# One pair of weights first, 66 pieces of attention alone on all PSUM banks, then FFN passes with the other weights converted under them

## The chip, the cores and the metric

The kernel runs on one core of a Trainium2 chip. The time is the device time of one execution in microseconds. Before the change it is 1069.12 us, the median of three runs (1068.13 to 1069.79).

## The reference: local and global attention, then an ELU feed-forward layer

```python
# q_l, k_l, v_l: (8, 8, 512, 64); q_g, k_g, v_g: (8, 8, 32, 64); w_in: (512, 2048); w_out: (2048, 512); all float32
s_g = scale * matmul(q_g, concat([k_g, k_l]).T)           # 32 global rows of each head see everything
out_g = matmul(sm(s_g), concat([v_g, v_l]))
s_ll = where(abs(i - j) <= 32, scale * matmul(q_l, k_l.T), -1e9)   # local rows see a band
s_l = concat([scale * matmul(q_l, k_g.T), s_ll])          # and the 32 global keys
out_l = matmul(sm(s_l), concat([v_g, v_l]))
x = concat([out_g, out_l]) as (4608 tokens, 512)
h = x @ w_in
g = where(h > 0, h, exp(min(h, 0)) - 1)
return g @ w_out
```

The weights arrive as eight-byte numbers (read as pairs of int32) and are turned into float32 and then into two float16 parts by the kernel itself.

## The kernel before

**Attention** is one generator of pieces (lines 357 to 559). A batch has ten slots: two global ones ("g", the 32 global queries of four heads against all keys) and eight local ones ("l", 128 local queries of four heads). Each slot takes four pieces, named S, T, U and V. Piece S of a local slot multiplies queries and keys (L434, `stage_s`), VectorE adds the mask and takes the maximum (L445), ScalarE takes the exponential (L452), VectorE and GpSimd normalise (L456, L457, L459). Two slots later pieces T and U transpose the probabilities on TensorE (L470) and copy them out of PSUM (L473), and one slot later still piece V multiplies them with the values (L489), whose result ScalarE copies to `xr` (L493). A global slot has the products of L385 and the softmax of L393 to L407. All of these use the PSUM pool `ps_a`, four banks. Eight batches make 80 slots and 323 pieces.

**The FFN** works on 17 blocks of 256 tokens: two to each batch, and one (the last) of all global rows. For a block, `split_x` finds the largest element (a transpose on TensorE, L101, then small VectorE steps) and writes the float16 parts `xh` (ScalarE, L285) and `xl` (VectorE, L288). A **pass** is one block with one pair of the 16 slices of 128 hidden units: 24 matmuls of L213 into PSUM `h`, the ELU (L221 and L222 on ScalarE, L223 on GpSimd, L228 on VectorE), its two float16 parts (L230, L231), and two passes later 12 matmuls of L255 into PSUM `acc`. That is 8 passes to a block and 136 in all. `h` and `acc` have two banks each, so that the eight banks are 2 + 2 + 4. A pass is eight steps of the generator `ffn_stream`.

**The weights** are converted in 16 units: for each of the eight pairs one unit of `w_in` and one of `w_out` (`unit`, L124). A unit loads 1 MB (L129, L132), and then runs steps on ScalarE (L141, L154 or none, L165), GpSimd (L142) and VectorE (L146, L147, L149, L152 for `w_in`, small steps, L168); a unit of `w_in` also has a transpose on TensorE (L101, the tile `cm`). The pairs come in groups: "a" is pair 0, "b" pair 1, "c" pairs 2 and 3, "d" pairs 4 to 7. When a group is converted, `tables` makes its scale tables (one transpose of `wm_a`, `wm_b` and so on, L101); with "d" comes "f", the table of all pairs. Until "f" exists, a block is done group by group: the partial sum of a group goes to DRAM (`od`, L267), and the next group loads it (L248) and adds it (L263). Afterwards a block goes through all eight pairs at once.

**The order.** The main loop (L571) takes the pieces of attention in turn. At piece i it starts a unit of a group where `CONV` says so (group "a" from piece 0 every 4 pieces, "b" from 22 every 6, "c" from 38 every 4, "d" from 54 every 4), and then as many FFN steps as `pace` asks for: none up to piece 30, then a ramp to piece 70, and from there 3.2 steps a piece (128 steps to the 40 pieces of a batch). Work that is deferred (`defer`) stands a number of ticks later; a tick is one piece or one FFN step. Every engine runs its instructions in the order that this gives, with some local reordering by the scheduler; all loads and stores go through one queue, SP's.

Of the kernel before, what the change touches and what calls it, by code (L numbers as in the profile page):

```python
# [10 lines left out]
F32 = mybir.dt.float32  # L11
# [10 lines left out]
DM, DF = 512, 2048  # L22
# [11 lines left out]
FFN0, FFN1, FFNLAG = 30, 70, 42  # L34
CONV = {"a": (0, 4), "b": (22, 6), "c": (38, 4), "d": (54, 4)}
# [11 lines left out]
def attn_ffn(ctx: ExitStack, tc: tile.TileContext, qT, qgT, kT, vT, w_in, w_out, mask, out):  # L47
# [36 lines left out]


# [28 lines left out]
    def load_weights(group):  # L114
        lo, hi = GROUPS[group]
        for p in range(lo, hi):
            for m in range(2):
                unit(m, p)
                yield
        defer(9, lambda: tables(group))  # L120
        if hi == NP:
            defer(10, lambda: tables("f"))

    def unit(m, p):  # L124
# [48 lines left out]
        lag = 3 if m else 12 if now[0] < 4 else 6  # L173
# [26 lines left out]
    def ffn_stream():  # L200
# [127 lines left out]
        left = 0  # L328
        while left <= NBL:
            load()  # L330
            job = job or choose()
            if job is None:
                yield True
                continue
            cur, job = job, None
            group, blk = cur[:2]
            lo, hi = GROUPS[group]
            for p in range(lo, hi):
                load()
                yield from ffn1(cur, p)  # L340
                if len(pend) > LAG2:
                    yield from ffn2()
                if p == hi - 1:
                    job = choose()
            if group in "df":
                del xs[blk]
                left += 1
# [9 lines left out]
    def attention():  # L357
# [69 lines left out]
        def stage_s(st, g, t):  # L427

            sp = [ps_a.tile([P, 512], F32, name="pa") for _ in range(2)]
# [35 lines left out]
        def stage_t(st, g, t, j):  # L465
# [6 lines left out]
            copy = nc.vector.tensor_copy if "f" in tab or (j and "a" in tab) else nc.scalar.copy  # L472
            copy(st["pt", g, t][:, 2 * j:2 * j + 2, :, 0:P], tp.rearrange("p (r i q) -> p r i q", r=2, i=2))  # L473

        def stage_v(st, g, t):
# [7 lines left out]
            pv = ps_a.tile([P, 512], F32, name="pa")  # L483
# [78 lines left out]
    spb = 4 * 10  # L562
    per = 2 * NP * 8
    f = ffn_stream()
    lw = [(load_weights(g), *CONV[g]) for g in CONV]
    done = 0

    def pace(i):
        return (i - FFNLAG) / spb * per

    for i, _ in enumerate(attention()):  # L571
        for units, first, step in lw:
            if i >= first and (i - first) % step == 0:
                next(units, None)
        want = pace(i) if i >= FFN1 else pace(FFN1) * (i - FFN0) / (FFN1 - FFN0)
        if done >= want:
            tick()
        while done < want:
            if next(f):
                tick()  # L580
                break
            done += 1
            tick()
# [60 lines left out]
```

## Time and profile before

| | |
|---|---|
| three runs | 1068.13, 1069.12, 1069.79 us |
| profiled execution | 1068.29 us, its span 1066.2 us |
| busy: PE / DVE / ACT / POOL | 994.4 / 568.4 / 526.0 / 296.4 us |
| mean granted TensorE clock | 0.965 |
| moved between DRAM and the core | 81.78 MB |

PE is TensorE, DVE VectorE, ACT ScalarE, POOL GpSimd; PEclk is the granted clock of TensorE as a share of full speed. "Busy" of PE is the union of its matmuls, at whatever clock they ran.

### The profile page before, as it was taken

How to read it: one execution, taken by the hardware profiler on the slowest of the kernel's cores; microseconds unless marked ns; L12 is line 12 of the kernel's file. 1: busy time of each engine (PE TensorE's matmuls, PEld its weight loads, DVE VectorE, ACT ScalarE, POOL GpSimd, SP SyncE). 2: the span in 40 equal slices, each digit the busy share in tenths (PEclk: the TensorE clock that was granted, in tenths of full speed). 3: DMA queues.
4: the chain of work that ended last, by engine and by line, in shares of the span. 5: the costliest groups of instructions: out<-in, count | busy, mean ns of one | idle time of the engine just before them, and what ended most of it. 6: DMA issues, size and time to landing. Idle time of an engine off the chain costs nothing.

```text
span 1066.2 us, 18867 instructions
## 1 busy us (share of the span) xinstructions
PE 994.4 (93%) x7182; PEld 690.5 (65%) x7182; DVE 568.4 (53%) x1669; ACT 526.0 (49%) x1246; POOL 296.4 (28%) x549
## 2 busy tenths in 40 slices
PE   5686985999999999999999999999999999999996
PEld 4464653666666766766676766676676767676663
DVE  5889689753465545454545455544555454433221
ACT  4666566653344445544544455444554454444342
POOL 3463524251222222222222132222222222211110
PEclk7886897999999999999999999999999999999998
DMA  7555356321143101310022102210131000000000
GB/s 289 163 168 193 128 194 227 90 91 44 50 144 120 45 21 65 95 45 26 31 76 82 52 11 94 80 46 14 65 101 41 20 31 22 20 21 20 1 20 21
DMA packets 39154, 81.78 MB, mean 77 GB/s; under 512 B 3864, under 2 KB 5912, under 8 KB 39064
## 3 DMA queue, kind: packets, MB, share of 16 engines
q1 hardware_dynamic: 39064, 80.58, 23.0%
q8 instruction: 57, 0.93, 0.4%
q14 instruction: 33, 0.27, 0.1%
HBM read 65.36 MB, written 15.20 MB: 76 GB/s over the span
## 4 chain that ended last, share of the span: by engine, by line
PE 77%; DVE 12%; ACT 5%; POOL 3%; issue 2%; DMA 1%; SPq 0%; POOLq 0%; ACTq 0%; DVEq 0%
PE h L213 32%; PE acc L255 29%; PE pa L489 6%; PE pa L434 4%; PE pa L470 4%; DVE p L445 2%; ACT p L452 2%; PE pa L385 2%; DVE cu L147 1%; POOL g L223 1%; DVE g L228 1%; DVE cu L149 1%; POOL p L459 1%; DVE gl L231 1%; ACT xh L285 1%
## 5 line engine op out<-in xcount | busy, mean ns | idle before, releaser
L213 PE MATMUL h<-xh,winh 128*128 128x256 f16 x1088 | 298.4, 275 | 17.0 <-ACT xh L285 15.9
L213 PE MATMUL h<-xl,winh 128*128 128x256 f16 x1088 | 298.3, 274 | 3.4 <-DVE xl L288 3.4
L213 PE MATMUL h<-xh,winl 128*128 128x256 f16 x1088 | 298.3, 274 | 0.0
L213 PEld LDWEIGHTS <-winh 128*128 128x128 f16 x2176 | 211.3, 98 | 58.9 <-issue 15.4
L255 PE MATMUL acc<-wouth,gh 128*128 128x512 f16 x544 | 206.8, 380 | 1.0 <-ACT o L266 1.0
L255 PE MATMUL acc<-woutl,gh 128*128 128x512 f16 x544 | 206.2, 379 | 0.0
L255 PE MATMUL acc<-wouth,gl 128*128 128x512 f16 x544 | 206.2, 379 | 0.0
L459 POOL TENSOR_SCALAR p<-p,sm 128x224 f32<-128x224 f32 x256 | 125.2, 507 | 265.8 <-ACT g L221 135.2
L223 POOL TENSOR_SCALAR g<-g,xs 128x512 f32<-128x512 f32 x136 | 95.8, 704 | 339.6 <-ACT g L222 324.1
L230 ACT CAST gh<-g 128x512 f16<-128x512 f32 x136 | 83.9, 617 | 207.4 <-DVE g L228 207.3
L228 DVE SCALAR_TENSOR_TENSOR g<-h,kk_f,g 128x512 f32<-128x512 f32 x104 | 78.1, 751 | 194.5 <-POOL g L223 194.4
L452 ACT ACTIVATE p<-p,m 128x224 f32<-128x224 f32 x256 | 120.1, 471 | 100.2 <-DVE m L448 99.9
L255 PEld LDWEIGHTS <-gh 128*128 128x128 f16 x1088 | 101.7, 98 | 93.0 <-issue 14.6
L221 ACT ACTIVATE g<-h,xs 128x512 f32<-128x512 f32 x136 | 92.7, 682 | 132.1 <-PE h L213 127.5
L231 DVE TENSOR_TENSOR gl<-g,gh 128x512 f16<-128x512 f32 x136 | 94.9, 698 | 45.0 <-ACT gh L230 44.0
L213 PEld LDWEIGHTS <-winl 128*128 128x128 f16 x1088 | 107.1, 98 | 18.0 <-issue 4.8
L445 DVE CUSTOM_DVE_ANT_0 p<-pa,msk 128x224 f32<-128x224 f32 x256 | 87.6, 384 | 24.5 <-PE pa L434 24.5
L255 PEld LDWEIGHTS <-gl 128*128 128x128 f16 x544 | 53.2, 98 | 63.7 <-issue 1.1
L470 PE MATMUL pa<-ident,p 128*128 128x128 f32 x512 | 79.7, 282 | 9.7 <-ACT pt L425 4.5
L222 ACT ACTIVATE g<-g 128x512 f32<-128x512 f32 x136 | 85.7, 630 | 3.6
L473 DVE COPY pt<-pa 128x512 f32<-128x512 f32 x110 | 74.7, 679 | 23.4 <-PE pa L470 22.4
L489 PE MATMUL pa<-pt,v 128*64 128x160 f32 (+2 forms) x1024 | 85.4, 311 | 0.6 <-DVE xglob L500 0.3
(148 smaller groups left out, 968.3 us busy)
## 6 DMA issues: line engine op xcount, KB each, us to landing
v<-vT SPq DMA_DIRECT2D x64, 256.0 KB, 2.7
k<-kT SPq DMA_DIRECT2D x32, 448.0 KB, 4.2
out<-o SPq DMA_DIRECT2D x34, 256.0 KB, 2.0
raw<-w_in SPq DMA_DIRECT2D x8, 1024.0 KB, 5.5
q<-qT SPq DMA_DIRECT2D x32, 256.0 KB, 4.8
raw<-w_out SPq DMA_DIRECT2D x8, 1024.0 KB, 5.2
od<-o SPq DMA_DIRECT2D x24, 256.0 KB, 2.1
o<-od SPq DMA_DIRECT2D x24, 256.0 KB, 3.0
```

The lines of the kernel that those rows point to most:

```text
L213: nc.tensor.matmul(h[:, j, :], wt[:, c, f], xt[:, c, :], start=k == 0, stop=k == 11)
L221: nc.scalar.activation(g, hf, AF.Relu, scale=sc[:, p:p + 1])
L222: nc.scalar.activation(g, g, AF.Exp, scale=-1.0)
L223: nc.gpsimd.tensor_scalar(g, g, -1.0, sc[:, NP + p:NP + p + 1], ALU.add, ALU.mult)
L228: nc.vector.scalar_tensor_tensor(out=g, in0=hf, scalar=kk[:, p:p + 1], in1=g, op0=ALU.mult, op1=ALU.max)
L231: defer(1, lambda: nc.vector.tensor_sub(gl, g, gh))
L255: nc.tensor.matmul(acc[t], gt[:, s], wt[:, f, :], start=p == first and j == 0 and k == 0, stop=p == last and j == 1 and k == 2)
L445: nc.vector.tensor_tensor_reduce(out=p[:, 0:KW], in0=sp[r][:, j * KW:(j + 1) * KW], in1=msk[:, mi, :], op0=ALU.add, op1=ALU.max, scale=1.0 ...
L452: nc.scalar.activation(ps[i][:, 0:KW], ps[i][:, 0:KW], AF.Exp, bias=m[:, 1, i:i + 1], scale=scale, accum_out=s[:, 0, i:i + 1])
L459: nc.gpsimd.tensor_scalar(ps[i][:, 0:KW], ps[i][:, 0:KW], s[:, 1, i:i + 1], 1.0, ALU.mult, ALU.mult)
L470: nc.tensor.transpose(tp[:, (2 * r + i) * P:(2 * r + i + 1) * P], ps[2 * j + r][:, i * P:(i + 1) * P], ident)
L489: nc.tensor.matmul(pv[64 * r:64 * r + 64, j * GW:j * GW + w], v[keys, 2 * j + i, r, :], pt[keys, 2 * j + r, i, 0:w], start=i == 0, stop=i ...
```

## The change: where conversions, attention and FFN steps stand

The first pair (group "a") is converted at pieces 0 and 4 as before. Up to piece 58 nothing else is converted, and up to piece 66 no FFN step is taken; `lead` is true for this time. While it is, piece S takes its two banks from `acc` in every second slot, piece V takes its bank from `h`, and VectorE copies only the second half of the transposed probabilities. `ffn_stream` meanwhile only splits the blocks that are ready. From piece 58 on, a counter starts the next unit after every 14 credits: a piece gives 2, an FFN step 1. The pace is 180 FFN steps between pieces 66 and 112, and 670 between 112 and 320. After the lead and until table "f" exists, ScalarE copies both halves of the transposed probabilities (before, VectorE took one of them once "a" was there). The scale tables are deferred by 14 and 15 ticks behind the start of a group's last unit (before: 9 and 10 behind the unit that followed). The work itself is the same: 323 pieces, 136 passes, 16 units, four blocks that are done group by group.

```diff
-FFN0, FFN1, FFNLAG = 30, 70, 42
-CONV = {"a": (0, 4), "b": (22, 6), "c": (38, 4), "d": (54, 4)}
+PACE = ((0, 0), (66, 0), (112, 180), (320, 850))
+CONV = 14
...
+    lead = [True]
...
                 unit(m, p)
+                if (m, p) == (1, hi - 1):
+                    defer(14, lambda: tables(group))
+                    if hi == NP:
+                        defer(15, lambda: tables("f"))
                 yield
-        defer(9, lambda: tables(group))
-        if hi == NP:
-            defer(10, lambda: tables("f"))
...
-        lag = 3 if m else 12 if now[0] < 4 else 6
+        lag = 3 if m else 10 if lead[0] else 6
...
+        while lead[0]:
+            load()
+            yield True
         while left <= NBL:
...
-            sp = [ps_a.tile([P, 512], F32, name="pa") for _ in range(2)]
+            if lead[0] and np_[0] % 8 == 0:
+                sp = [ps_o.tile([P, DM], F32, name="acc") for _ in range(2)]
+            else:
+                sp = [ps_a.tile([P, 512], F32, name="pa") for _ in range(2)]
...
-            copy = nc.vector.tensor_copy if "f" in tab or (j and "a" in tab) else nc.scalar.copy
+            copy = nc.vector.tensor_copy if "f" in tab or (j and lead[0]) else nc.scalar.copy
...
-            pv = ps_a.tile([P, 512], F32, name="pa")
+            if lead[0]:
+                pv = ps_h.tile([P, 2, BLK], F32, name="h").rearrange("p a b -> p (a b)")
+            else:
+                pv = ps_a.tile([P, 512], F32, name="pa")
...
-    spb = 4 * 10
-    per = 2 * NP * 8
     f = ffn_stream()
-    lw = [(load_weights(g), *CONV[g]) for g in CONV]
-    done = 0
+    units = (u for g in "abcd" for u in load_weights(g))
+    done = credit = 0
     def pace(i):
-        return (i - FFNLAG) / spb * per
+        for (i0, d0), (i1, d1) in zip(PACE, PACE[1:]):
+            if i < i1:
+                break
+        return d0 + (d1 - d0) * (i - i0) / (i1 - i0)
+    def convert(n):
+        nonlocal credit
+        credit += n
+        if credit >= CONV:
+            credit -= CONV
+            next(units, None)
     for i, _ in enumerate(attention()):
-        for units, first, step in lw:
-            if i >= first and (i - first) % step == 0:
-                next(units, None)
-        want = pace(i) if i >= FFN1 else pace(FFN1) * (i - FFN0) / (FFN1 - FFN0)
+        lead[0] = i < PACE[1][0]
+        if i in (0, 4):
+            next(units)
+        elif i >= PACE[1][0] - 8:
+            convert(2)
+        want = pace(i)
+        if lead[0]:
+            next(f)
         if done >= want:
             tick()
         while done < want:
...
             done += 1
+            convert(1)
             tick()
```

Lines of the changed kernel lie 4 to 14 further down: L101 is L105 there, L213 is L218, L434 is L445, L445 is L456, L470 is L481, L489 is L503.

How this moves the instructions is shown at three places. The first is TensorE's list in the first batch, one local slot (S, the transposes T and U, and V of an earlier slot). Before:

```order
L434 MATMUL pa<-k,q 128x224 x4
L419 MATMUL pa<-ident,pg 128x128
L470 MATMUL pa<-ident,p_81 128x128 x2
L470 MATMUL pa<-ident,p_82 128x128 x2
L470 MATMUL pa<-ident,p_83 128x128 x2
L470 MATMUL pa<-ident,p_84 128x128 x2
L489 MATMUL pa<-pt,v 64x160 x8
```

And now:

```order
L445 MATMUL acc<-k,q 128x224 x4
L427 MATMUL pa<-ident,pg 128x128
L481 MATMUL pa<-ident,p_85 128x128 x2
L481 MATMUL pa<-ident,p_86 128x128 x2
L481 MATMUL pa<-ident,p_87 128x128 x2
L481 MATMUL pa<-ident,p_88 128x128 x2
L503 MATMUL h<-pt,v 64x160 x2
```

The products of S stand in `acc` here and the values of V in `h`; the transposes keep `pa`.

The second place is VectorE's list where the first unit of pair 1 is converted (`cu` is the weight being built, `p` and `m` are the masked scores and maxima of attention). Before, it stands among attention pieces of the first batch:

```order
L146 TENSOR_SCALAR cu<-cu 128x1024
L445 ISA p_85,m<-pa,msk 128x224
L445 ISA m 128x1
L147 SCALAR_TENSOR_TENSOR cu<-raw,cu 128x1024
L456 TENSOR_SCALAR sm<-sm 128x4
L445 ISA p_86,m<-pa,msk 128x224
L445 ISA m 128x1
L149 SCALAR_TENSOR_TENSOR cu<-raw,cu 128x1024
L457 RECIPROCAL sm<-sm 128x4
L445 ISA p_87,m<-pa,msk 128x224
L445 ISA m 128x1
L152 TENSOR_REDUCE cm<-cu 128x1
```

Now most units stand among passes (`g`, `gl`), as this one of pair 2, well behind the lead:

```order
L151 TENSOR_SCALAR cu<-cu 128x1024
L152 SCALAR_TENSOR_TENSOR cu<-raw,cu 128x1024
L233 SCALAR_TENSOR_TENSOR g<-h,kk_a,g 128x512
L154 SCALAR_TENSOR_TENSOR cu<-raw,cu 128x1024
L236 TENSOR_TENSOR gl<-g,gh 128x512
L233 SCALAR_TENSOR_TENSOR g<-h,kk_b,g 128x512
L166 TENSOR_SCALAR cm<-cm 128x1
L100 TENSOR_SCALAR pwo<-cm 128x1
L168 RECIPROCAL cm<-pwo 128x1
L169 TENSOR_SCALAR cm<-cm 128x1
L236 TENSOR_TENSOR gl<-g,gh 128x512
```

The units have moved from between attention pieces to between the steps of passes.

The third place is ScalarE's list in the steady part, where a block is split (`xh`) and passes follow (L221 before, L226 now; `xs` holds the scales of the pass's block, with its number). Before:

```order
L230 CAST gh_4851<-g_4847 128x512
L493 COPY xr_4879<-pa_4881 128x2x128
L285 ACTIVATE xh_4813<-xr_4222,xm_4223 128x1024
L399 ACTIVATE pg_4926,sg_4929<-pa_4920,mg_4928 128x272
L399 ACTIVATE pg_4926,sg_4929<-pa_4921,mg_4928 128x272
L221 ACTIVATE g_4948<-h_4901,xs_4897 128x512
```

Here the next pass (scales `xs_4897`) is already the first of the block just split, `xh_4813`. Now:

```order
L290 ACTIVATE xh_4496<-xr_3964,xm_3965 128x1024
L271 ACTIVATE o_3995<-acc_3993,xs_3796 128x512
L226 ACTIVATE g_4628<-h_4597,xs_4412 128x512
L227 ACTIVATE g_4628<-g_4628 128x512
L507 COPY xr_4636<-pa_4638 128x2x128
L235 CAST gh_4632<-g_4628 128x512
L407 ACTIVATE pg_4676,sg_4679<-pa_4670,mg_4678 128x272
L407 ACTIVATE pg_4676,sg_4679<-pa_4671,mg_4678 128x272
L433 COPY pt_4707<-pa_4708 128x4x32
L226 ACTIVATE g_4729<-h_4689,xs_4412 128x512
```

The passes behind the split still belong to an older block (`xs_4412`), six of them in all, before the first pass on `xh_4496` (scales `xs_5062`): the FFN runs further behind the attention than it did.

## The prediction

> **What bounds the kernel now.** I read the page first, then busy times by stretch, then the waits of each stretch. The page's first part and slices:
>
> ```profile
> span 1066.2 us, 18867 instructions
> PE 994.4 (93%) x7182; PEld 690.5 (65%) x7182; DVE 568.4 (53%) x1669; ACT 526.0 (49%) x1246; POOL 296.4 (28%) x549
> PE   5686985999999999999999999999999999999996
> DVE  5889689753465545454545455544555454433221
> PEclk7886897999999999999999999999999999999998
> ```
>
> A slice is 26.7 us. From the ninth on TensorE (PE) is full at full clock; the first eight (213 us) are the only place with something to win, and there VectorE (DVE) is the fuller engine and PE's clock is down. Two rows of the timeline mark the edges of that stage: the transposes for the first pair's table and for the table of all pairs, behind which every pair is converted.
>
> ```profile
> 29.70 0.45 PE L101 MATMUL pa<-ident,wm_a 128*128 128x128 f32 x1 [3.83 <-DVE wm_a L184]
> 223.31 0.27 PE L101 MATMUL pa<-ident,wm_f 128*128 128x128 f32 x1
> ```
>
> Busy times between these marks, and behind them:
>
> ```profile
> core 0: us, PE busy (x) PEld busy (x) DVE busy (x) ACT busy (x) POOL busy (x), PEclk, DMA share, GB/s
> 29.70:114.70 85.00, 64.43 (x392) 46.33 (x393) 72.06 (x228) 52.75 (x135) 43.91 (x65) 0.76 0.53 177
> 114.70:151.70 37.00, 35.43 (x241) 23.06 (x239) 25.72 (x51) 21.78 (x40) 9.36 (x16) 1.00 0.41 135
> 151.70:187.00 35.30, 20.67 (x141) 14.86 (x142) 34.06 (x102) 23.05 (x55) 18.96 (x31) 0.84 0.73 242
> 187.00:223.30 36.30, 33.87 (x251) 24.39 (x250) 27.34 (x92) 23.20 (x56) 13.65 (x27) 0.97 0.29 85
> 223.30:1056.20 832.90, 824.00 (x6113) 571.11 (x6111) 392.07 (x1122) 389.98 (x925) 199.25 (x394) 1.00 0.16 50
> 1056.20:1066.20 10.00, 0.00 (x0) 0.00 (x0) 0.00 (x0) 0.67 (x1) 0.00 (x0) 0.68 0.18 53
> ```
>
> The stage from 29.7 to 223.3 takes 193.6 us; DVE is busy for 72.06 + 25.72 + 34.06 + 27.34 = 159.2 us of it and PE for 154.4. They take turns at being the bound: passes run back to back without conversions from 114.7 to 151.7 (PE 96%, DVE 70%), conversions with little PE work stand behind (DVE 96%, PE 59%). PE's share and DVE's together are 1.61, 1.65, 1.55 and 1.69 in the four rows. Behind 223.3 PE is busy for 824.0 of 832.9 us, and the last 10.0 us hold no matmul. PE's waits, first for the window 29.7 to 223.3, the last row for what follows 224:
>
> ```profile
> PE pa L101 <- DVE cm L152: 10.3, 4, 4.4
> PE h L213 <- ACT xh L285: 7.1, 3, 4.1
> PE h L213 <- DVE xl L288: 3.4, 2, 1.9
> ...
> PE h L213 <- ACT xh L285: 8.8, 6, 1.5
> ```
>
> So the steady part loses 8.8 us, six times 1.5, in passes that begin the moment their block is split.
>
> **The change, part by part.** The end is set by PE: the time is when the table of all pairs stands (T), plus PE's remaining work, its remaining waits, 10.0 us of tail, and the 1068.29 − 1066.2 = 2.1 us of the profiled execution outside its span. Its own time is 0.8 us under the median of the three runs.
>
> *What PE has done by T.* Counted in the two TensorE lists up to the row of `wm_f`, the changed kernel has 101 matmuls of L213 more (410 for 309), 48 of L255 more (180 for 132), 3 local slots more of S, 3 of T and U, and 2 of V. Their price at full clock:
>
> ```profile
> 1040.55 2.62 PE h L213 x24
> 1032.75 2.59 PE acc L255 x12
> 205.50 1.03 PE L434 MATMUL pa<-k,q 64*128 64x224 f32 x8
> 207.96 1.06 PE L470 MATMUL pa<-ident,p 128*128 128x128 f32 x8 [1.18 <-DVE xglob L500]
> 209.26 1.21 PE L489 MATMUL pa<-pt,v 128*64 128x160 f32 x16
> 210.40 2.10 PE L385 MATMUL pa<-k,qg 128*128 128x272 f32 x8
> ```
>
> 101 × 2.62/24 = 11.0; 48 × 2.59/12 = 10.4; 3 × 1.03 + 3 × 1.06 + 2 × 1.21 = 8.7; with four small transposes (0.13 each) 30.6, say 31 us. Behind T then remain 824.0 − 31.0 = 793.0 us.
>
> *The waits behind T.* Now six passes of an older block stand between a split and its first use (the third place shown): over 30 us of PE work covers what lacked 1.5 us. I take the 8.8 us as gone, with 0 in their place; if the cover fails they cost 8.8 again.
>
> *T: VectorE's work.* All 16 units are done by T in both. The rows of what differs:
>
> ```profile
> L445 DVE CUSTOM_DVE_ANT_0 p<-pa,msk 128x224 f32<-128x224 f32 x256 | 87.6, 384 | 24.5 <-PE pa L434 24.5
> L473 DVE COPY pt<-pa 128x512 f32<-128x512 f32 x110 | 74.7, 679 | 23.4 <-PE pa L470 22.4
> L228 DVE SCALAR_TENSOR_TENSOR g<-h,kk_f,g 128x512 f32<-128x512 f32 x104 | 78.1, 751 | 194.5 <-POOL g L223 194.4
> L231 DVE TENSOR_TENSOR gl<-g,gh 128x512 f16<-128x512 f32 x136 | 94.9, 698 | 45.0 <-ACT gh L230 44.0
> L263 DVE SCALAR_TENSOR_TENSOR o<-acc,xs,o 128x512 f32<-128x512 f32 x24 | 17.7, 744 | 6.4 <-PE acc L255 6.4
> L473 ACT COPY pt<-pa 128x512 f32<-128x512 f32 x18 | 10.5, 583 | 6.3 <-PE pa L470 6.2
> L452 ACT ACTIVATE p<-p,m 128x224 f32<-128x224 f32 x256 | 120.1, 471 | 100.2 <-DVE m L448 99.9
> ```
>
> Between the two marks DVE has 12 masked maxima more (12 × 0.384 = 4.6), 7 copies fewer (−7 × 0.679 = −4.8), 4 passes more (4 × (0.751 + 0.698) = 5.8), 4 partial sums more (4 × 0.744 = 3.0) and some 15 small steps, about 2 us: 10.6 more, 159.2 + 10.6 = 169.8 us. ScalarE gains 12 exponentials, about 11 copies and 4 passes, some 20 us on the 120.8 of the four rows: 141 us, no bound. GpSimd has 86 us in the same rows and gains under 10.
>
> *T: TensorE's work.* 154.4 + 31 = 185.4 us at the clocks of the rows above. At full clock the first row's 64.43 us at 0.76 would be 15.5 us shorter, the third's 20.67 at 0.84 3.3, the fourth's 33.87 at 0.97 1.0: 165.6 us at best. What takes the clock down is seen in slices of 4 us:
>
> ```profile
> 72.00:76.00 4.00, 4.00 (x41) 3.07 (x38) 3.44 (x7) 4.00 (x9) 2.83 (x4) 1.00 0.15 35
> 88.00:92.00 4.00, 1.26 (x9) 1.01 (x11) 4.00 (x9) 1.13 (x1) 2.22 (x4) 0.79 0.78 258
> 92.00:96.00 4.00, 4.00 (x20) 2.95 (x16) 2.92 (x8) 1.32 (x5) 1.95 (x2) 0.50 0.93 337
> ```
>
> A slice in which PE hardly worked, because it waited for a conversion on DVE, is followed by one at 0.50. In the lead there are no conversions between pieces 4 and 58, and later every unit has passes beside it, so I take three quarters of the 19.8 us back: 170.5 us. [...]
>
> *T: the sum.* 169.8 + 170.5 = 340.3 us. The four rows reach 1.55 to 1.69 together per microsecond. The two lowest are those in which conversions stand alone among attention pieces; the changed order has passes with them, so I take 1.67, the mean of the two rows in which passes dominate: 203.8 us. The stage before 29.7 keeps its instructions, but two products and one V are now in front of the mark: 30.5. T = 234.3. **The sum: 234.3 + 793.0 + 0 + 10.0 + 2.1 = 1039.4 us, with the 0.8 to the median 1040.** With 1.55 and the old clocks, (169.8 + 185.4)/1.55 = 229.2: 1066. With 1.69 and full clock, 198.5: 1035. With DVE at the 96% of the third row, 169.8/0.965 = 176.0: 1012.
>
> *The eight banks.* I give them nothing of their own: PE's waits above name conversions and splits, no bank. [...]
>
> *The queues.* SP has the same loads and stores, but loads of weights now stand among the stores of partial sums, each waiting for its pass, with the loads of values behind them.
>
> ```profile
> SPq L267 <- ACT o L266: 35.4, 5, 17.7
> ...
> L141 ACT ACTIVATE cu<-raw 128x1024 f32<-128x1024 f32 x16 | 18.4, 1147 | 5.5 <-DMA raw<-w_out 5.4
> ```
>
> Before, the stores held SP for 35.4 us, and still ScalarE waited only 5.4 us for weights, since two units are buffered. I take no change; the far end is one such longest hold, 17.7 us, in full on the path: 1057. On GpSimd the passes' L223 now queues behind conversions more often; at 86 of 194 us busy it has room.
>
> **The rivals.**
> *The clock stays low in the lead, and it is slower.* From the `wm_a` mark to the first L213 the changed TensorE list holds 9.5 S, 9 T and U, 8 V, two global products and 13 small transposes: 9.8 + 9.5 + 9.7 + 4.2 + 1.7 = 35 us at full clock. The nearest row, with attention and conversions:
>
> ```profile
> 29.70:67.00 37.30, 27.87 (x177) 20.70 (x178) 31.68 (x107) 24.86 (x71) 17.59 (x28) 0.78 0.58 198
> ```
>
> At its PE share of 75% the lead takes 35/0.75 = 47 us at full clock, 60 at its clock of 0.78 (+13: 1053), 94 at half clock (+47: 1087). It ends slower than before if the lead's mean clock is under 0.6. For it: attention alone has less PE work per slot than anything later. Against: slices as full as 72 to 76 stood at 1.00.
> *Passes and conversions take turns.* If a pass waits for DVE behind a unit and DVE then waits for PE, the joint share falls; at 1.55 and the old clocks it is 1066, as above, and under 355.2/234.9 = 1.51 slower than before.
> *VectorE is kept full.* 1012, as above; against it, neither stretch dominated by passes had DVE over 75%.
> *The change does less than it says:* the 8.8 us stay, or go to another wait: 1048.
>
> **How the numbers follow.** Forecast, 1028 to 1052 (with the 8.8 us on either side): 0.58. Low clock or turn-taking that still leaves a gain, 1052 to 1066: 0.17. VectorE nearly full, 1012 to 1028: 0.11. About the same: 0.04. Slower: 0.10 (clock 0.06, turns 0.04). A measurement tells about 0.2% (2.1 us) from no change; so faster 0.86, same 0.04, slower 0.10. The range 1020 to 1064 leaves out the 0.14 of the last two, and a part of each edge.
>
> **What would show it.** Right: no L213 before about 75 us and a clock near 1.00 from 35 us on; the `wm_f` transpose at 225 to 245 us; DVE and PE together about 1.67 between the marks; the wait of L213 for `xh` absent behind it. Wrong: `wm_f` past 263 us (no gain is left there); clocks of 0.50 in the lead; ScalarE waiting for `raw` by more than some 10 us; new waits of PE in the steady part.

## The result, and the profile after

The changed kernel takes 1036.64 us, the median of four runs (1033.16 to 1037.28), against 1068.62 us (1067.23 to 1069.79) for the kernel before: a ratio of 0.9695, 95% interval 0.9669 to 0.972. 1040 was predicted. The profiled execution took 1037.27 us, 2.1 of them outside its span. One execution on record was slow, one of the twelve of experiment e6 below (1300.15 us at a mean clock of 0.745): it counts in e6's median, not in its ratio, and without it that median is 1066.84.

The page of the changed kernel, first part and the slices of two engines and of the clock:

```profile
span 1035.2 us, 18899 instructions
PE 988.9 (96%) x7182; PEld 683.8 (66%) x7182; DVE 565.5 (55%) x1657; ACT 529.0 (51%) x1258; POOL 301.4 (29%) x549
...
PE   6998888989999999999999999999999999999996
...
DVE  5788798884464555455554555455555455422221
...
PEclk7799998999999999999999999999999999999998
```

PE is as busy as before in sum (988.9 us for 994.4); the span is shorter because the first nine slices, taken together, are fuller. The same two edges, in the timeline:

```profile
30.20 0.47 PE L105 MATMUL pa<-ident,wm_a 128*128 128x128 f32 x1
...
232.79 0.27 PE L105 MATMUL pa<-ident,wm_f 128*128 128x128 f32 x1
```

`wm_f` stands 9.5 us later than before (232.79 for 223.31), and the span still ends 31.0 us earlier, so 40.5 us have left what lies behind it. Busy times between the edges as a whole, in five parts, and behind them:

```profile
core 0: us, PE busy (x) PEld busy (x) DVE busy (x) ACT busy (x) POOL busy (x), PEclk, DMA share, GB/s
30.20:232.80 202.60, 177.23 (x1235) 121.96 (x1235) 170.93 (x512) 140.68 (x342) 97.72 (x157) 0.93 0.54 175
30.20:74.50 44.30, 43.00 (x315) 31.00 (x314) 33.51 (x160) 32.90 (x114) 20.71 (x47) 0.89 0.44 148
74.50:112.00 37.50, 31.89 (x231) 21.98 (x232) 31.68 (x101) 29.77 (x74) 23.66 (x35) 0.95 0.68 220
112.00:153.00 41.00, 34.50 (x253) 24.04 (x251) 37.25 (x98) 28.97 (x55) 21.03 (x32) 0.96 0.59 191
153.00:193.00 40.00, 31.25 (x195) 20.36 (x195) 34.91 (x62) 21.83 (x35) 19.98 (x23) 0.91 0.52 167
193.00:232.80 39.80, 36.60 (x245) 24.57 (x244) 33.58 (x96) 27.20 (x64) 12.35 (x23) 0.96 0.49 154
232.80:1025.20 792.40, 792.18 (x5878) 549.37 (x5877) 376.46 (x1067) 373.33 (x882) 192.38 (x372) 1.00 0.15 48
1025.20:1035.20 10.00, 0.65 (x3) 0.10 (x1) 0.00 (x0) 0.81 (x2) 0.00 (x0) 0.72 0.17 52
```

Three things are to be read here. Between the edges PE and VectorE together are busy for 177.23 + 170.93 = 348.2 us in 202.6: 1.72 per microsecond, where it was 1.62. Behind the lead (the second to the fifth part) VectorE is at 84 to 91% and PE at 78 to 92%: no part is left to one of them alone, as two of the four were before. And behind `wm_f` PE is idle for 0.2 us of 792.4. Its waits say the same, the first three rows over the window of the edges, the last over all that follows 233:

```profile
PE h L218 <- DVE g L233: 9.1, 2, 5.1
PE pa L105 <- DVE cm L157: 8.1, 4, 3.0
PE pa L481 <- ACT pt L433: 3.6, 3, 2.7
...
PE h L218 <- DVE g L233: 0.2, 1, 0.2
```

The wait for `xh`, 8.8 us before, is gone from the steady part. The largest that is left stands where a pass needs PSUM `h`, which is released by the ELU (L233), and this stands on VectorE behind steps of a conversion; the next is for the maximum `cm` of a conversion itself.

### The profile page after: what moved, and what is told of

Its sections match the earlier page's. It is cut to its first block, busy times and chain, and to the rows that moved or that the text cites. A ratio compares the mean times of both kernels' runs of the same rounds, so it can differ in the third digit from the quotient of the medians.

```text
span 1035.2 us, 18899 instructions
## 1 busy us (share of the span) xinstructions
PE 988.9 (96%) x7182; PEld 683.8 (66%) x7182; DVE 565.5 (55%) x1657; ACT 529.0 (51%) x1258; POOL 301.4 (29%) x549
## 4 chain that ended last, share of the span: by engine, by line
PE 84%; DVE 6%; ACT 3%; issue 2%; POOL 2%; DMA 1%; SPq 0%; ACTq 0%; POOLq 0%; DVEq 0%
PE h L218 32%; PE acc L260 31%; PE pa L503 6%; PE pa L445 5%; PE pa L481 5%; PE pa L393 3%; POOL g L228 1%; DVE cu L154 1%; DMA k<-kT 1%; DVE p L456 1%; DMA raw<-w_out 1%; DVE g L233 1%; PE h L503 1%; PE pa L427 1%; PE acc L445 1%
## 5 line engine op out<-in xcount | busy, mean ns | idle before, releaser
L218 PE MATMUL h<-xh,winh 128*128 128x256 f16 x1088 | 299.0, 275 | 9.4 <-DVE g L233 9.3
L218 PE MATMUL h<-xl,winh 128*128 128x256 f16 x1088 | 298.6, 275 | 0.2 <-DVE xl L293 0.2
L218 PE MATMUL h<-xh,winl 128*128 128x256 f16 x1088 | 298.5, 274 | 0.0
L218 PEld LDWEIGHTS <-winh 128*128 128x128 f16 x2176 | 211.1, 99 | 68.8 <-issue 20.2
L260 PE MATMUL acc<-wouth,gh 128*128 128x512 f16 x544 | 207.3, 381 | 0.3 <-DVE o L268 0.3
L260 PE MATMUL acc<-wouth,gl 128*128 128x512 f16 x544 | 207.0, 381 | 0.0
L260 PE MATMUL acc<-woutl,gh 128*128 128x512 f16 x544 | 206.8, 380 | 0.0
L228 POOL TENSOR_SCALAR g<-g,xs 128x512 f32<-128x512 f32 x136 | 100.7, 740 | 362.5 <-ACT g L227 340.3
L470 POOL TENSOR_SCALAR p<-p,sm 128x224 f32<-128x224 f32 x256 | 123.2, 499 | 225.5 <-DVE sm L468 149.6
L233 DVE SCALAR_TENSOR_TENSOR g<-h,kk_f,g 128x512 f32<-128x512 f32 x104 | 78.1, 751 | 197.0 <-POOL g L228 196.9
L260 PEld LDWEIGHTS <-gh 128*128 128x128 f16 x1088 | 102.9, 98 | 92.4 <-issue 12.0
L226 ACT ACTIVATE g<-h,xs 128x512 f32<-128x512 f32 x136 | 92.8, 682 | 103.7 <-PE h L218 103.4
L236 DVE TENSOR_TENSOR gl<-g,gh 128x512 f16<-128x512 f32 x136 | 94.3, 694 | 43.7 <-ACT gh L235 42.0
L218 PEld LDWEIGHTS <-winl 128*128 128x128 f16 x1088 | 107.2, 99 | 13.6 <-issue 0.3
L260 PEld LDWEIGHTS <-gl 128*128 128x128 f16 x544 | 53.3, 98 | 64.5 <-issue 0.8
L456 DVE CUSTOM_DVE_ANT_0 p<-pa,msk 128x224 f32<-128x224 f32 x228 | 78.1, 384 | 22.3 <-PE pa L445 22.1
L481 PE MATMUL pa<-ident,p 128*128 128x128 f32 x512 | 80.6, 282 | 6.5 <-ACT pt L433 3.6
L484 DVE COPY pt<-pa 128x512 f32<-128x512 f32 x98 | 66.7, 681 | 22.8 <-PE pa L481 22.3
L481 PEld LDWEIGHTS pa<-ident,p 128*128 128x128 f32 x512 | 62.0, 145 | 19.5 <-issue 7.3
```

The costliest lines, as they stand in the source:

```text
L218: nc.tensor.matmul(h[:, j, :], wt[:, c, f], xt[:, c, :], start=k == 0, stop=k == 11)
L226: nc.scalar.activation(g, hf, AF.Relu, scale=sc[:, p:p + 1])
L228: nc.gpsimd.tensor_scalar(g, g, -1.0, sc[:, NP + p:NP + p + 1], ALU.add, ALU.mult)
L233: nc.vector.scalar_tensor_tensor(out=g, in0=hf, scalar=kk[:, p:p + 1], in1=g, op0=ALU.mult, op1=ALU.max)
L236: defer(1, lambda: nc.vector.tensor_sub(gl, g, gh))
L260: nc.tensor.matmul(acc[t], gt[:, s], wt[:, f, :], start=p == first and j == 0 and k == 0, stop=p == last and j == 1 and k == 2)
```

## The experiments

Each edit is made to the changed kernel unless another is named, and each was timed in five rounds beside the kernel before on the same chip. The local reordering of the scheduler answers to every edit and moves some rows of all engines, and the runs of one kernel lie up to 6.3 us apart (e3), those of e7 9.7, so differences under some 2 us are not read.

| run | median, us | ratio to before, interval | `wm_f` at, us |
|---|---|---|---|
| the change | 1036.64 | 0.9695 (0.9669 to 0.972) | 232.8 |
| e1, four banks | 1036.38 | 0.9693 (0.968 to 0.9705) | 231.9 |
| e2, passes close behind | 1044.10 | 0.9769 (0.9755 to 0.9783) | 231.6 |
| e3, before, held back | 1061.45 | 0.9929 (0.9911 to 0.9946) | 226.7 |
| e4, conversions from piece 22 | 1038.52 | 0.9715 (0.9703 to 0.9728) | 192.4 |
| e5, one conversion step less | 1022.52 | 0.9568 (0.9546 to 0.9589) | 217.0 |
| e6, without lead | 1067.08 | 0.9978 (0.9967 to 0.9989) | 212.4 |
| e7, credits of pieces alone | 1051.45 | 0.9819 (0.979 to 0.9848) | 224.7 |
| e9, later transposes | 1036.84 | 0.9698 (0.9676 to 0.9719) | 232.6 |
| e10, old copy rule | 1036.75 | 0.9705 (0.9686 to 0.9724) | 232.8 |
| e11, short lead | 1041.10 | 0.9745 (0.9726 to 0.9763) | 194.8 |
| e12, low parts on GpSimd | 1037.06 | 0.9702 (0.9683 to 0.9721) | 235.3 |
| e13, low parts twice | 1042.77 | 0.9749 (0.9726 to 0.9771) | 237.8 |

None of those that do the whole work is faster than the change by more than can be read.

**e1: the banks.** S and V of the lead take their banks from `pa`, as before.

```diff
-            if lead[0] and np_[0] % 8 == 0:
-                sp = [ps_o.tile([P, DM], F32, name="acc") for _ in range(2)]
-            else:
+            if True:
                 sp = [ps_a.tile([P, 512], F32, name="pa") for _ in range(2)]
...
-            if lead[0]:
-                pv = ps_h.tile([P, 2, BLK], F32, name="h").rearrange("p a b -> p (a b)")
-            else:
+            if True:
                 pv = ps_a.tile([P, 512], F32, name="pa")
```

> The changed kernel (1036.6 us) with pieces S and V of the lead on the four banks of pa again, all else the same. My theory gave the extra banks nothing: 1036.6 within 2 us, the lead (30.2 to 73.7 in the changed trace) as long as there, PE about 97% busy in it. Rival: with four banks PE waits in the lead for copies out of PSUM, its share falls to the 75% that the kernel before had from 29.7 to 67; 43 us of work at 75% take 57 in place of 44: 1049.

1036.38 us: the eight banks are worth nothing that can be read.

**e2: the passes close behind the splits again.** The pace catches up with that of before by piece 150; up to `wm_f` it stays as it is.

```diff
-PACE = ((0, 0), (66, 0), (112, 180), (320, 850))
+PACE = ((0, 0), (66, 0), (112, 180), (150, 346), (320, 890))
```

> The changed kernel with the FFN brought close behind the attention again: the pace rises between pieces 112 and 150 to the line of the kernel before (346 steps at 150, 890 at 320); nothing differs up to the table of all pairs. My theory: of the kernel before's 8.8 us of waits of L218 for xh (1.5 us for each block whose passes begin right behind its split) five come back, so 7.4 us: 1044, with the row PE h L218 <- ACT xh L290 at 7 to 8 us. Rival: the change's gain is all in the first 233 us, the waits are made up elsewhere: 1036.6 within 2.

1044.10 us, 7.5 above the change, with `wm_f` where it was. The waits of PE behind 232, engine and line, what was waited for, us in all, times, longest:

```profile
PE h L218 <- ACT xh L290: 7.3, 5, 1.5
PE h L218 <- DVE g L233: 0.2, 1, 0.2
```

The old wait is back at its old length of 1.5 us a time, and the time has grown by what it sums to.

**e3: the same, from the other side.** The kernel before, with its pace held back by 48 steps (six passes) between pieces 112 and 160.

```diff
-        return (i - FFNLAG) / spb * per
+        return (i - FFNLAG) / spb * per - 48 * min(max((i - 112) / 48, 0), 1)
```

> The kernel before (1068.6 us) with 48 FFN steps held back between pieces 112 and 160 and never caught up until the attention ends; the first 223 us stay as they are. My theory: the 8.8 us of waits for xh vanish and nothing takes their place: 1060 (1058 to 1062). Rival: the steps held back leave PE waiting for attention pieces, or the waits move: 1066 to 1070.

1061.45 us, 7.9 below the kernel before beside it (1069.32). So about 8 of the 32 us come from the distance between a split and its first pass, and a line of the old kernel would have given them. The other 24 us are the business of the stretch between the edges.

**e4: conversions in the lead.** The credits run from piece 22, so that units stand among attention alone as well.

```diff
-        elif i >= PACE[1][0] - 8:
+        elif i >= 22:
```

> The changed kernel with units converted from piece 22 on (a piece gives 2 credits of 14) in place of piece 58: five or six of the 14 remaining units now run under attention alone. By the lists PE has 43 us less work done when the table of all pairs stands, VectorE some 27 us less; so the kernel is level if that table stands at 190 us. My theory (PE and DVE busy together 1.72 per us where conversions lie under passes, 1.55 to 1.61 where under attention alone): the stretch holds 278 us of both and takes 174 us at 1.60, the table stands at 204, 1051 (1045 to 1055). Rival: only the amounts count, not what lies beside what: 162 us at 1.72, the table at 192, 1039.

1038.52 us: my theory, 1051, falls, and the rival holds. `wm_f` comes 40 us earlier, with less of PE's work done by then, and the stretch is shared as well as in the change, (136.22 + 141.88)/161.6 = 1.72:

```profile
30.80:192.40 161.60, 136.22 (x911) 92.86 (x911) 141.88 (x414) 111.97 (x264) 79.50 (x118) 0.90 0.55 180
```

Conversions under attention alone cost nothing that can be read. Whether they start at piece 22 or at 58 is worth 2 us.

**e5: less VectorE work.** VectorE's step L154, one of its large steps on `cu` in a conversion (five in a unit of `w_in`, four in one of `w_out`), stands for pair 0 only: 14 instructions less (the three lowest bits of the float32 weights of pairs 1 to 7 are left out).

```diff
-            nc.vector.scalar_tensor_tensor(out=ui, in0=low, scalar=29, in1=ui,
-                                           op0=ALU.logical_shift_right, op1=ALU.bitwise_or)
+            if p == 0:
+                nc.vector.scalar_tensor_tensor(out=ui, in0=low, scalar=29, in1=ui,
+                                               op0=ALU.logical_shift_right, op1=ALU.bitwise_or)
```

> The changed kernel without one VectorE step of the conversion (L154, which puts in the three lowest bits of a weight) for pairs 1 to 7: 14 instructions of 1.22 us, 17 us less on VectorE before the table of all pairs, nothing less on PE (the lists have PE 1 us earlier there). It tells which engine sets the 202.6 us of that stretch, where PE is busy 87% and VectorE 84%. My theory, PE and VectorE hold each other up and only their joint time per us (1.72) counts: 17/1.72 = 10 us less, 1027 to 1028. Rival A, VectorE alone is the bound: 17 us less, 1020. Rival B, PE alone is the bound: 1036.

1022.52 us, 14.1 less. The row between the edges:

```profile
30.80:217.00 186.20, 167.30 (x1228) 116.61 (x1228) 154.05 (x496) 140.33 (x339) 84.58 (x157) 0.96 0.57 190
```

VectorE is busy for 16.9 us less, and PE for 9.9 us less although it does nearly the same work (0.8 us less of it): its clock is 0.96 instead of 0.93. The two are again shared at (167.30 + 154.05)/186.2 = 1.73. By median it is 14.1/16.9 = 0.83 us for each microsecond of VectorE, between the shared time that I expected (1027 to 1028) and VectorE as the bound alone (1020). Before the later runs I took this for a price of VectorE's load as such.

**e6: the credits without the lead.** The old ramp of the pace, the old copy rule and lags, four banks, and no lead; the units are still started by credits, from piece 22.

```diff
-PACE = ((0, 0), (66, 0), (112, 180), (320, 850))
+PACE = ((0, 0), (30, 0), (70, 90), (112, 224), (320, 890))
...
-    lead = [True]
+    lead = [False]
...
-        lag = 3 if m else 10 if lead[0] else 6
+        lag = 3 if m else 12 if now[0] < 4 else 6
...
-            copy = nc.vector.tensor_copy if "f" in tab or (j and lead[0]) else nc.scalar.copy
+            copy = nc.vector.tensor_copy if "f" in tab or (j and "a" in tab) else nc.scalar.copy
...
-        lead[0] = i < PACE[1][0]
...
-        elif i >= PACE[1][0] - 8:
+        elif i >= 22:
             convert(2)
...
-        if lead[0]:
-            next(f)
```

> The kernel before (1069 us) with one thing of the change: units start by credits (14 of them; 2 from a piece, 1 from an FFN step) from piece 22 on, in place of fixed pieces. No lead, no extra banks, the FFN steps from piece 30 and on the old line, close behind the attention. The last run showed that conversions may stand under attention alone without loss. New theory: what cost time before was that conversions stood at fixed pieces, so that they paused while FFN steps that were due ran off without a piece (114.7 to 151.7 us, VectorE 70% busy) and came close together afterwards; with credits they go on. Then the joint time reaches about 1.72 per us: 147.5 + 143 = 290.5 us take 169, the table of all pairs stands at 199.5, 1055 (1052 to 1058; the 8.8 us of waits for xh stay). Rival, the lead is what does it: at the old 1.62 the stretch takes 179, 1066 (1063 to 1069).

1067.08 us: my theory, 1055, falls; the credits by themselves bring nearly nothing. The stretch, and PE's largest wait in it:

```profile
29.70:212.40 182.70, 140.50 (x922) 96.95 (x923) 149.97 (x414) 112.14 (x253) 84.41 (x119) 0.85 0.50 165
```

```profile
PE h L218 <- ACT xh L290: 9.3, 2, 6.3
```

Passes that begin on a block just split wait for the split, up to 6.3 us at a time, and the shared rate is 1.59 at a clock of 0.85, a little worse than in the kernel before (1.62 at 0.86). The waits for `xh` are 9.3 of the 42.2 us in which PE is idle here, so they are a part of the low rate, and not all of it.

**e7: the conversions paced by attention alone.** Five credits a piece, none for an FFN step.

```diff
-            convert(2)
+            convert(5)
...
             done += 1
-            convert(1)
             tick()
```

> The changed kernel with units started by pieces alone (5 credits a piece from piece 58, none from an FFN step): the same lead, banks and pace, 14 units in about the same pieces, but conversions pause where FFN steps run off without a piece. By the lists the table of all pairs has 157 us of VectorE and 153 us of PE work in front of it in the stretch, and 24 us more of PE behind it. New theory (steady conversion counts): the joint time falls to about the old 1.62, 191 us, the table at 222, 1050 (1045 to 1053). Rival, the amounts count and the lead gives the gain: 180.5 us, the table at 211, 1039.

1051.45 us, 14.8 above the change. Five of the six runs lie between 1050.74 and 1053.04 us, at mean clocks of 0.965 to 0.970; the sixth took 1043.38 us at 0.982, and in it only 6.7 of the 14.8 us are left. The row between the edges, and PE's longest wait, in the run of 1053.04 us:

```profile
30.40:224.70 194.30, 157.39 (x1052) 105.57 (x1052) 157.21 (x465) 124.71 (x299) 90.46 (x144) 0.87 0.50 165
```

```profile
PE h L218 <- ACT winh L170: 7.9, 2, 6.8
```

The shared rate is back at 1.62 and the clock at 0.87, about the values of the kernel before (1.62 and 0.86). The edit changes only when units start: without the credits of FFN steps none starts while FFN steps run in a row, and several can follow one another among pieces. In the trace this is a small difference: behind the lead, the first VectorE steps of the units (L151) stand 7.2 to 18.6 us apart in the change and 4.0 to 19.9 here; between the edges of the kernel before they stand 5.9 to 34.1 us apart. And e6, at 6.6 to 19.0, has the low rate too. So when the units start is shown to matter, in five runs of six; that it matters because they bunch is argued and not shown.

**e9: later transposes of `cm`.** PE waits for these 8.9 us in all; they are put 10 ticks behind everywhere.

```diff
-        lag = 3 if m else 10 if lead[0] else 6
+        lag = 3 if m else 10
```

> The changed kernel with the transposes for the maximum of a w_in unit (cm, L105) always 10 ticks behind the unit's start, in place of 6 outside the lead. In the changed trace PE waits 8.9 us, five times, at these transposes for VectorE's maximum, and stands in order there. My theory: the waits shrink by half or more, VectorE gets passes to work on meanwhile: 1032 to 1034. Rival: PE waits as long at the next instruction that needs VectorE (9.3 us for the release of h stand there already): 1036.6 within 2.

1036.84 us: the rival holds. PE's waits:

```profile
PE h L218 <- DVE xm L289: 5.1, 1, 5.1
...
PE acc L260 <- DVE o L268: 3.8, 2, 3.6
PE pa L105 <- DVE cm L157: 3.2, 3, 2.0
```

The wait for `cm` falls from 8.9 to 3.2 us, and two others take its place. This wait was the name of what VectorE had not done yet, and not a cause of its own.

**e10: copies from ScalarE to VectorE.** The old copy rule alone. In the traces VectorE has 18 of these copies between the edges, for 9 in the change.

```diff
-            copy = nc.vector.tensor_copy if "f" in tab or (j and lead[0]) else nc.scalar.copy
+            copy = nc.vector.tensor_copy if "f" in tab or (j and "a" in tab) else nc.scalar.copy
```

> The changed kernel with the old rule for who copies the transposed blocks: VectorE has 19 rather than 9 of these copies up to the last table, 10 more of 0.68 us, 6.8 us of VectorE work in the stretch, taken off ScalarE. VectorE as the near bound of the stretch (0.83 us per us, as the run without the low bits showed): wm_f ends 5.6 us later, about 1042. PE and VectorE sharing the stretch at 1.72: 4 us later, 1040.5. If these copies were free where they stand: 1036.6.

1036.75 us, nothing, where 0.83 for each of the 6.8 us expected would have given 5.6.

```profile
30.90:232.80 201.90, 173.35 (x1237) 120.07 (x1238) 176.31 (x520) 136.32 (x333) 95.86 (x156) 0.94 0.53 176
```

VectorE has 5.4 us more, PE 3.9 less at a clock of 0.94, and the sum is shared at 1.73. The two nearly cancel, and part of PE's 3.9 us is the clock at the start of the lead, which was 1.00 here and 0.50 in the change (last section). So this run doesn't show by itself that the copies are free.

**e11: the lead cut to piece 30, with e4's credits.**

```diff
-PACE = ((0, 0), (66, 0), (112, 180), (320, 850))
+PACE = ((0, 0), (30, 0), (112, 180), (320, 850))
...
-        elif i >= PACE[1][0] - 8:
+        elif i >= 22:
```

> The kernel with the conversions from piece 22 on, with the lead (attention alone) cut to piece 30. What is to be done on PE and on VectorE up to the last table is nearly what it was in that kernel (125 and 174 us against 126 and 176 by the count of instructions), but the split blocks are used directly behind their splits. If the lead matters by the stock of split blocks that it leaves: PE and VectorE share the stretch at 1.60 instead of 1.72, wm_f ends about 11 us later than 192.4, at 203.5, and the whole takes about 1050. If only the amounts count: 1038.5, as without the cut.

1041.10 us: 3.2 above e4 by the ratios, under a third of what the lead was expected to be worth. The row of the stretch, and the waits in it:

```profile
31.00:194.80 163.80, 131.02 (x911) 89.25 (x910) 141.81 (x405) 115.14 (x263) 88.42 (x120) 0.92 0.56 184
```

```profile
PE h L218 <- ACT xh L290: 6.2, 2, 4.0
...
PE h L218 <- DVE xl L293: 3.3, 3, 1.4
```

The waits for splits are there, 6.2 and 3.3 us, where e4 has 2.2 for `xl` alone, so the stock of split blocks that a long lead leaves does take most of them away, and the shared rate is 1.67 without it. But the long lead isn't what separates e6 (1067) from the change: e11 has a short one and is 26 us below e6. About 9 of the 26 are the waits for `xh` behind `wm_f`, which e6 has again with the old pace (18.1 us in all, 9.3 of them ahead of it). The rest is `wm_f` itself, 17.6 us later in e6 (212.4 for 194.8). It isn't the amount of work: up to there e6 has run 312 matmuls of L218 and e11 311, 122 and 120 of L260, and as many pieces of attention. Nor does the ramp of the pace explain it, which starts at piece 30 in both and asks for 90 steps by piece 70 in e6 and 88 in e11. In those rows e6 has the lower clock (0.85 for 0.92) and 8.2 us more on VectorE. What else the two differ in is the short lead with its early splits and banks, the copy rule and the lag of the first unit; banks and copy rule gave nothing alone in e1 and e10, and no run takes one of these from e11 to e6, so what makes up the 17.6 us stays open.

**e12: the low parts on GpSimd.** The subtraction of L236 is given to GpSimd up to table "f".

```diff
-                defer(1, lambda: nc.vector.tensor_sub(gl, g, gh))
+                sub = nc.vector if "f" in tab else nc.gpsimd
+                defer(1, lambda: sub.tensor_sub(gl, g, gh))
```

> The changed kernel with the subtraction that makes the low part of the activation on GpSimd instead of VectorE up to the last table: 16 instructions of about 0.70 us, 11 us of VectorE work less in the stretch. By 0.83 us per us: wm_f 9 us earlier, 1027.5; by the shared time at 1.72: 1030. Rival: GpSimd takes longer for one of them than VectorE and its queue of transpositions and loads stands behind it, so that the second matmul of the FFN waits for the low part: 1036.6 or more.

1037.06 us, no gain. The stretch:

```profile
31.40:235.30 203.90, 179.66 (x1228) 123.64 (x1228) 170.12 (x495) 141.11 (x340) 116.82 (x173) 0.92 0.53 174
```

VectorE has lost 16 instructions and is as busy as before, 170.1 us for 170.9. Groups of the window 30 to 235, busy us and mean ns of one. In the change:

```profile
L154 DVE SCALAR_TENSOR_TENSOR cu<-raw,cu 128x1024 int32<-128x1024 int32 x14 | 18.2, 1303 | 0.0
L152 DVE SCALAR_TENSOR_TENSOR cu<-raw,cu 128x1024 int32<-128x1024 int32 x14 | 18.2, 1298 | 0.1
L236 DVE TENSOR_TENSOR gl<-g,gh 128x512 f16<-128x512 f32 x16 | 10.9, 684 | 0.3 <-ACT gh L235 0.2
...
L157 DVE TENSOR_REDUCE cm<-cu 128x1 f32<-128x1024 f32 x7 | 8.5, 1212 | 0.1
```

With the low parts on GpSimd (its own row last):

```profile
L154 DVE SCALAR_TENSOR_TENSOR cu<-raw,cu 128x1024 int32<-128x1024 int32 x14 | 20.7, 1481 | 0.0
L152 DVE SCALAR_TENSOR_TENSOR cu<-raw,cu 128x1024 int32<-128x1024 int32 x14 | 20.3, 1447 | 0.1
...
L157 DVE TENSOR_REDUCE cm<-cu 128x1 f32<-128x1024 f32 x7 | 8.5, 1213 | 0.1
...
L237 POOL TENSOR_TENSOR gl<-g,gh 128x512 f16<-128x512 f32 x16 | 26.1, 1629 | 20.6 <-ACT gh L235 19.1 <-DVE m L457 1.5
```

The work takes 1.63 us on GpSimd for 0.68 on VectorE, and meanwhile two of VectorE's own steps with two inputs take 14 and 11% longer (1481 for 1303 ns, 1447 for 1298), while the reduction with one input stays as it was (1213 for 1212). These two alone give back 4.6 of the 10.9 us; the rest is spread over other groups, of which not all grew (L173, with two inputs as well, went from 1280 to 1437 ns for `woutl` and from 1516 to 1292 for `winl`). So not every step with two inputs got longer, and that the work on GpSimd is what lengthened the others was not shown: no run takes the two apart.

**e13: VectorE's low parts twice.** The opposite: more of these instructions, beside the conversions; the traces have 32 between the edges, for 16 in the change.

```diff
-                defer(1, lambda: nc.vector.tensor_sub(gl, g, gh))
+                defer(1, lambda: [nc.vector.tensor_sub(gl, g, gh) for _ in range(1 if "f" in tab else 2)])
```

> The changed kernel in which VectorE makes the low part of the activation twice up to the last table: 17 more instructions of 0.69 us, 11.7 us of VectorE work added in the passes, no ScalarE or TensorE work and no step of a conversion. If VectorE's load bounds the stretch (0.83 us per us, as the run without the low bits would have it): 9.7 us later, 1046.5; by a shared time of PE and VectorE at 1.72: 6.8 us, 1043.5. If what the run without the low bits took away counts as a link of a conversion's chain, and VectorE work beside the chain fits into its idle time, as 5.4 us of copies did: 1036.6 to 1038.5.

1042.77 us, 5.8 more by the ratios.

```profile
31.80:237.80 206.00, 178.62 (x1256) 123.75 (x1256) 183.64 (x527) 140.97 (x340) 91.80 (x156) 0.95 0.53 172
```

VectorE is busy for 12.7 us more. Half a microsecond for each is neither the 0.83 of e5 nor nothing: the nearest of the three expectations is the shared rate (6.8).

## Why the prediction came out

*T* came at 232.8, predicted at 234.3, with two errors that cancel. VectorE was sized well: 170.93 us for 169.8. PE was not: "I take three quarters of the 19.8 us back" gave 170.5, and 177.23 were measured, so only 185.4 − 177.2 = 8.2 of 19.8 came back. The clock was at 0.50 for 10.2 us at the start of the lead and later for 3.4 us at each of five places (from 101.2, 118.3, 155.8, 172.9 and 213.9 us), each of these five behind 3.4 us in which PE worked for less than 1 us (0.67, 0.05, 0.00, 0.68 and 0.99). So the argument that "every unit has passes beside it" didn't hold: stretches with hardly any work of PE were left. On the other side the rate of "1.67, the mean of the two rows in which passes dominate" was too low: 1.72 was reached. With the measured busy times and 1.67 the stretch would be 348.2/1.67 = 208.5 us, 5.9 too long; with the predicted ones and 1.718 it would be 340.3/1.718 = 198.1, 4.5 too short. That T came within 1.5 us is luck in part. The two errors are not independent either: PE's busy time is counted at the clock at which it ran, so a lower clock raises the busy time (matmuls of L218 start 0.21 us apart from 118.4 to 121.4 us, at 0.50, and 0.11 from 121.9 to 122.4, at 1.00), and in the same span the rate with it; PE's predicted 170.5 us in the 202.6 would have made the rate 1.685. The term that failed is the clock.

*Why the rate is higher.* The rows of before mixed stretches with conversions and stretches with passes. The change and seven of the runs that keep its long lead and count pieces and FFN steps (e1, e2, e4, e5, e9, e10, e12) lie between 1.71 and 1.73, with VectorE's work from 142 to 176 us; the eighth, e13, reaches 1.76. The three that give up one of the two are lower: e11 with the short lead at 1.67, e7 with pieces alone at 1.62, e6 without lead at 1.59. Within this order the rate is nearly the stable number, and the length of the stretch is what both engines have to do, at PE's clock, divided by it. The rate describes an order; what in the orders of e6 and e7 makes theirs low was not found. "VectorE is kept full", the rival of 1012, isn't reached: VectorE is at 84% in the change and at 89% in e13.

*What a microsecond of VectorE is worth* came out differently in three places: 0.83 in the middle of a conversion (e5), 0.46 beside the passes (5.8/12.7, e13), nothing measurable for copies (e10). The three differ in the clock too (0.96, 0.95 and 0.94 for the change's 0.93), so that the place alone sets the price is not shown. In e5 the clock gave its part: PE's 9.9 us and VectorE's 16.9 divided by 1.72 are 15.6 of the 16.4 us by which the stretch was shorter. Why the clock recovered there and hardly in e13 (0.95 for 0.93) isn't settled.

*PE behind T*: 792.18 + 0.65 = 792.8 us for 793.0, so the 31 us of work moved ahead were counted rightly. *The waits*: 0 for the 8.8 us, as taken; e2 and e3 show the price from both sides, 7.5 and 7.9. *Tail and rest*: 9.3 us behind the last matmul for 10.0, and 2.1 as before. *Banks*: nothing, shown by e1. *The SP queue*: no change, as taken; ScalarE's step that waits for weights waited 3.3 + 2.1 = 5.4 us for them, as before:

```profile
L146 ACT ACTIVATE cu<-raw 128x1024 f32<-128x1024 f32 x16 | 18.4, 1151 | 5.6 <-DMA raw<-w_out 3.3 <-DMA raw<-w_in 2.1
```

ScalarE had 140.7 us for 141; GpSimd 97.7, a little more than the "under 10" added to 86.

*The lead.* The first L218 of the change stands at 73.7 us, about as expected, but "a clock near 1.00 from 35 us on" was wrong by 5 us, and the rival's PE share of 75% wrong by more: PE was busy for 43.0 of 44.3 us at a mean clock of 0.89. Attention alone fed PE nearly without gaps here, so the clock rival had no ground to stand on behind 40 us; what it lost, it lost ahead of that. That the lead is what makes the gain was never a term of the sum, and e11 shows that its length is worth some 3 us.

So the 31.0 us between the profiled executions are 40.5 less behind `wm_f` (31.2 us of PE's work done earlier, 8.6 of waits, 0.7 of tail) and 9.5 more ahead of it. The first was read from the lists of instructions, the second from the rows; the experiments show the waits' 8 us and, for when the units start, some 15 in five runs of e7 and 6.7 in the sixth. Which part of the new order gives the rest of the 24 us ahead of `wm_f` stays open.

## What to carry to other kernels

Where two engines share a stage, read what both have to do and how much of both together a stretch has got done per microsecond so far, not which wait stands longest: one wait that was moved came back under other names (e9), and the rate stayed within 1.71 to 1.76 in eight edits. It falls when the order changes in a way that isn't understood yet (e6, e7, e11), so try a new order before trusting it. Starting slow side work by a counter of the main engine's steps, of all kinds of them, was better than by some of them (e7), but doesn't do by itself (e6). Keep a producer several consumers ahead once the stage is steady (e2, e3). Giving work of the full engine to an idle one brought nothing where some of the full one's other instructions got longer, two steps by 14 and 11% (e12).

## What the runs showed of the hardware

*The clock fell to half behind gaps in PE's work, at the three places below for 3.4 us each.* Rows of the changed kernel, each of this length, three falls one behind the other:

```profile
97.80:101.20 3.40, 0.67 (x5) 0.35 (x4) 1.89 (x4) 3.40 (x12) 1.28 (x2) 1.00 0.75 278
101.20:104.60 3.40, 3.40 (x12) 1.76 (x11) 2.51 (x13) 1.48 (x4) 1.73 (x4) 0.51 0.70 209
104.60:108.00 3.40, 3.40 (x29) 2.79 (x28) 2.06 (x13) 3.40 (x11) 1.51 (x7) 0.99 1.01 282
114.90:118.30 3.40, 0.05 (x1) 0.05 (x1) 1.71 (x3) 0.88 (x3) 3.19 (x5) 1.00 0.00 0
118.30:121.70 3.40, 3.40 (x17) 2.35 (x17) 3.28 (x8) 2.38 (x4) 0.00 (x0) 0.50 0.13 8
121.70:125.10 3.40, 3.40 (x21) 1.92 (x20) 2.64 (x4) 2.30 (x4) 0.00 (x0) 1.00 0.89 319
152.40:155.80 3.40, 0.00 (x0) 0.00 (x0) 3.40 (x6) 2.03 (x9) 1.41 (x1) 1.00 0.25 77
155.80:159.20 3.40, 2.58 (x12) 1.77 (x12) 3.40 (x11) 1.83 (x3) 0.45 (x2) 0.51 0.00 0
159.20:162.60 3.40, 3.40 (x23) 2.12 (x22) 3.40 (x11) 2.19 (x3) 3.40 (x7) 0.99 0.75 178
```

Here a row in which PE worked for 0.67, 0.05 or 0.00 us is followed by one at 0.50 or 0.51, and that by one at 0.99 or 1.00. So, as an estimate from them, each of these gaps cost twice: its idle time, and up to 1.7 us of work (half of 3.4) in the next row. Not every stretch ahead of a fall was so empty: the one before the next rows, 26.2 to 29.6, had 1.98 us of work and was followed by 0.50 too. And the return took longer elsewhere: the kernel before stayed at 0.50 from 90.3 to 114.2 us, while PE was busy for 17.21 of 23.90 us. So it did at the start of the lead, 10.2 us at half clock with PE busy throughout:

```profile
29.60:39.80 10.20, 10.20 (x38) 6.70 (x39) 6.75 (x32) 6.37 (x19) 4.49 (x9) 0.50 0.34 126
39.80:43.20 3.40, 3.23 (x33) 2.36 (x31) 1.87 (x11) 3.40 (x16) 0.39 (x1) 1.00 0.38 105
```

That is an estimated 5 us of PE's work (half of 10.2), but not shown to be 5 us of time: in the profiled execution of e10, whose order differs there by a few rows, the clock was 1.00 from 28 to 44 us, and `wm_f` stood at 232.8 and the time at 1037.36 us, as in the change. What decides the clock there wasn't tried.
